# Attention's prologue and first turn in another order, two squares on ScalarE, the reciprocal's transpose two chunks later, layer 1's low parts on VectorE

## The chip, the core and the metric

The kernel runs on one core of a Trainium2 chip. The core has a matrix engine (TensorE, PE in the profile; PEld is its weight load), VectorE (DVE), ScalarE (ACT), GpSimd (POOL) and a queue engine that only issues transfers (SyncE, SP). Each engine works through its own list of instructions in order and waits on semaphores for the others. The metric is device time of one execution in microseconds: the median of the runs.

## What is computed

```
q_n, k_n = rmsnorm(q, g_q), rmsnorm(k, g_k)          # q, k, v: 4 x 12 x 448 x 64
scores = q_n @ k_n^T / sqrt(64)
attn = exp(scores - rowmax);  attn = attn / (rowsum + 1e-9)
x = (attn @ v), heads side by side                   # 1792 x 768
x = ((x @ w_a) * (x @ w_b)) @ w_out                  # layer 0, d_ff 1536
x = (sigmoid(x @ w_gate) * (x @ w_val)) @ w_out      # layer 1, d_ff 1536
```

## The kernel before

Attention works on 24 pairs of heads. For a pair, `load` and `load_r` fetch q and k, `squares` squares them, `mean` sums and averages on VectorE, `rsqrt` takes a logarithm and an exponential on ScalarE, `newton` improves the result on VectorE with three small instructions, and `scale` multiplies q and k with it into `qkn` (n = 1 is k, n = 0 is q, n = 2 the remainders of both, of which q's go to `qrem`). `t_tr` transposes the scaled k (1) and q (0) on TensorE. Every result of the transpose is split in a high and a low part: `k_hi` and `q_hi` are ScalarE copies (k's carries the gain `G`), `k_lo` and `q_lo` VectorE subtractions, and `k_ends` are two small GpSimd copies. `s` makes the scores from high and low parts, three products each, `top` the row maxima on VectorE, `exp` the exponentials and their sums on ScalarE. `x_tr` transposes the exponentials, `x_out` copies them out of PSUM (ScalarE for z = 0, VectorE for z = 1), and `pv` multiplies with v. The normalisation goes round by DRAM: `rsum` takes the reciprocals of the sums on VectorE, `rsum_tr` transposes them on TensorE, `rsum_post` copies the row on ScalarE and stores it (`dr`), `rsum_get` of the next turn loads it back over 64 partitions (`rs`), and `norm` multiplies on VectorE.

No scheduler orders this. The order is written out by hand in three tables: `begin` is the prologue, `turns` is run once for each pair from 1 to 22 with offsets from the pair (so in turn i it makes the scores of pair i, the transposes and products of pair i - 1 and the scaled q and k of pairs i + 1 to i + 4), and `end` closes. An engine's list of instructions is what these tables give it. Squares and scaling of pair 0, and the scaling of pair 1, are on VectorE, of all others on GpSimd. `qkn` has one buffer, `tr` in PSUM three, the scores four. From turn 6 on, `decode` weaves the unpacking of layer 0's weights into each turn; its raw words arrive by SP's queue.

The two layers multiply by a seven-product scheme, every operand again split in high and low. `first_part` makes the gated products, `second_part` the product with w_out: 42 steps k (seven passes of six), each with six chunks on TensorE in layer 0, and behind each chunk a `tick`. A tick calls `step`, which prepares the operands of step k + 3 on VectorE and ScalarE (names d, wh, wl for weights, u, gh, gl for activations), and then takes one task from the list `after`. Behind passes 6 and 7 this list holds three additions (`more`) and three `finish`, whose `split` makes layer 1's operand: the high part by ScalarE, the low part (`xl`, 128x896) by GpSimd. The last two passes of layer 0 write into the same PSUM bank, so the first product of pass 4 has to wait for ScalarE's copy of pass 7 (line 1156).

Of the kernel before, what the change touches and what calls it, by code (L numbers as in the profile page):

```python
# [23 lines left out]
def attention_then_two_gated_mlps(  # L24
# [90 lines left out]
    def attention():  # L115
# [68 lines left out]

        def squares(i):
            d = st[i]
            first = i < 1
# [6 lines left out]
            w = 0 if first else D // 2
            while w >= 32:
                eng.tensor_tensor(out=sq[:, :, 0:w], in0=sq[:, :, 0:w], in1=sq[:, :, w:2 * w], op=ALU.add)
                w //= 2
            d["sq"] = sq if first else sq[:, :, 0:2 * w]
# [72 lines left out]
        def k_hi(i):  # L271
            d = st[i]
            KH, KL = (qk.tile([P, 512], F32R, tag=n, name=n) for n in ("KH", "KL"))
            if i == 0:
                nc.vector.scalar_tensor_tensor(
                    out=G, in0=gg[:, 0:1], scalar=1.0 / float(D) ** 0.5, in1=gg[:, 1:2], op0=ALU.mult, op1=ALU.mult
                )
# [172 lines left out]
        begin = (  # L450
            (load, 0), (load_r, -6), (load_r, -5), (load_r, -4), (load_r, -3), (load_g, 0), (load_r, -2),
            (load, 1), (squares, 0), (mean, 0), (rsqrt, 0), (newton, 0), (load, 2), (scale, 0, 1),
            (load_r, -1), (scale, 0, 0), (load_r, 0), (scale, 0, 2), (t_tr, 0, 1), (k_hi, 0), (squares, 1),
            (mean, 1), (t_tr, 0, 0), (rsqrt, 1), (k_lo, 0), (k_ends, 0), (newton, 1), (load, 3), (load_r, 1),
            (q_hi, 0), (q_lo, 0), (scale, 1, 1), (load_r, 2), (s, 0, 0), (scale, 1, 0), (scale, 1, 2),
            (s, 0, 1), (top, 0, 0), (load_v, 0), (load_v, 1), (t_tr, 1, 0), (squares, 2), (exp, 0, 0), (top, 0, 4),
            (q_hi, 1), (mean, 2), (t_tr, 1, 1), (exp, 0, 4), (q_lo, 1), (rsqrt, 2), (k_hi, 1), (top, 0, 1), (newton, 2),
            (exp, 0, 1), (top, 0, 5), (scale, 2, 1), (k_lo, 1), (k_ends, 1), (exp, 0, 5), (s, 0, 2), (s, 0, 3), (load, 4),
            (scale, 2, 0), (scale, 2, 2), (top, 0, 2), (load_r, 3), (exp, 0, 2), (top, 0, 6), (squares, 3),
            (exp, 0, 6), (top, 0, 3), (t_tr, 2, 1), (t_tr, 2, 0), (exp, 0, 3), (mean, 3), (k_hi, 2), (k_lo, 2),  # L460
            (rsqrt, 3), (q_hi, 2), (newton, 3), (q_lo, 2), (k_ends, 2),
        )
# [788 lines left out]
```

## Time and profile before

| what | us |
|---|---|
| median of three runs (1259.92 to 1262.04) | 1260.2 |
| the profiled execution | 1261.72 |
| its span, first to last instruction | 1259.9 |
| TensorE busy in the span | 1206.6 (96%) |
| VectorE busy | 941.0 (75%) |
| ScalarE busy | 653.0 (52%) |
| GpSimd busy | 183.8 (15%) |

The span is the time from the first to the last instruction, and 1.8 us lie around it. TensorE is busy nearly all the time, so a saving is read from the stretches in which it stands idle or runs at the lower of its clocks; the waits and the timeline show those, with the engine that ended each wait.

### The profile page before, as it was taken

Reading aid. Unit: us, or ns where it says so; the run is one execution under the profiler, and the core shown is the slowest. Engines: PE = TensorE matmul, PEld = TensorE weight load, DVE = VectorE, ACT = ScalarE, POOL = GpSimd, SP = SyncE. Lnnn points to the kernel's source line nnn. Section 1 sums busy time; section 2 is a strip of 40 time slices with the busy share of each in tenths; the row PEclk is TensorE's granted clock in tenths of the full one; section 3 lists DMA queues with packets and bytes.
Section 4 is the critical chain, followed back from the end, with each engine's and each line's share of the span. In section 5 each row is a group of like instructions: output and inputs, shape, how many; then the busy total and the mean of one; then the engine's idle time right before and its main releaser. Section 6 shows DMA issues by size and latency. Waiting matters only on the chain.

```text
span 1259.9 us, 18180 instructions
## 1 busy us (share of the span) xinstructions
PE 1206.6 (96%) x6414; PEld 1016.9 (81%) x6414; DVE 941.0 (75%) x1617; ACT 653.0 (52%) x1267; POOL 183.8 (15%) x250
## 2 busy tenths in 40 slices
PE   4999999999889999999999989989999999999997
PEld 3565665566778888888888878878888888999997
DVE  6787889873986777877557689976787777557583
ACT  3677788773554345334345546544445454445543
POOL 4564557720000000000002022000000000000000
PEclk8899999999899999999999999999999999999999
DMA  5234455425324555653875644123555655577573
GB/s 128 67 111 139 114 143 155 142 83 202 103 86 137 181 168 172 200 166 126 283 244 168 225 157 155 61 94 118 190 168 172 193 155 178 196 274 259 173 254 108
DMA packets 142026, 203.00 MB, mean 161 GB/s; under 512 B 23240, under 2 KB 116592, under 8 KB 141936
## 3 DMA queue, kind: packets, MB, share of 16 engines
q1 hardware_dynamic: 140816, 201.27, 50.6%
q8 instruction: 50, 0.82, 0.3%
q10 hardware_dynamic: 1120, 0.59, 0.2%
q14 instruction: 40, 0.33, 0.1%
HBM read 147.46 MB, written 54.35 MB: 160 GB/s over the span
## 4 chain that ended last, share of the span: by engine, by line
PE 80%; DVE 10%; ACT 4%; issue 2%; DMA 2%; POOL 1%; SPq 0%; ACTq 0%; DVEq 0%; POOLq 0%
PE mm L871 45%; PE mm L1123 10%; PE mm L1133 9%; PE pv L365 5%; PE s L305 5%; PE tr L336 3%; DVE xl L560 2%; DVE nm L311 2%; PE tr L254 1%; PE tr L333 1%; ACT gh L1040 1%; DVE d L630 1%; DMA d<-wd 1%; DVE wl L560 1%; DVE QL L269 1%
## 5 line engine op out<-in xcount | busy, mean ns | idle before, releaser
L871 PE MATMUL mm<-xh,wh 128*128 128x512 f32 (+1 forms) x1008 | 371.1, 368 | 9.5 <-ACT u L923 3.8
L871 PE MATMUL mm<-xl,wh 128*128 128x512 f32 (+1 forms) x1008 | 371.0, 368 | 5.5 <-DVE xl L560 5.5
L871 PE MATMUL mm<-xh,wl 128*128 128x512 f32 (+1 forms) x1008 | 372.0, 369 | 0.0
L560 DVE TENSOR_TENSOR wl<-d,wh 128x384 fp32r<-128x384 f32 x252 | 143.7, 571 | 161.1 <-ACT wh L718 100.2
L871 PEld LDWEIGHTS mm<-xh,wh 128*128 128x128 f32 x1008 | 191.1, 190 | 35.7 <-ACT u L923 4.4
L871 PEld LDWEIGHTS mm<-xl,wh 128*128 128x128 f32 x1008 | 191.1, 190 | 30.2 <-DVE xl L560 7.3
L871 PEld LDWEIGHTS mm<-xh,wl 128*128 128x128 f32 x1008 | 190.7, 189 | 21.3
L718 ACT CAST wh<-d 128x384 fp32r<-128x384 f32 x168 | 85.9, 511 | 167.3 <-DVE d L706 145.9
L1013 ACT CAST wh<-d 128x384 fp32r<-128x384 f32 x84 | 43.2, 514 | 150.0 <-DVE d L1010 54.3
L623 ACT ACTIVATE d<-raw 128x384 f32<-128x384 f32 x140 | 78.1, 558 | 65.0 <-DMA raw<-in_moe_w_a_dram 15.0
L323 ACT ACTIVATE P<-s,nm 128x448 f32<-128x448 f32 x168 | 104.9, 635 | 12.1 <-DVE nm L311 12.1
L311 DVE TENSOR_REDUCE nm<-s 128x1 f32<-128x448 f32 x168 | 97.3, 614 | 7.1 <-PE s L305 7.1
L1133 PE MATMUL mm<-wh,gh 128*128 128x384 f32 x294 | 98.8, 336 | 0.5 <-ACT ah L1156 0.3
L1133 PE MATMUL mm<-wl,gh 128*128 128x384 f32 x294 | 98.6, 335 | 0.0
L1133 PE MATMUL mm<-wh,gl 128*128 128x384 f32 x294 | 98.5, 335 | 0.0
L1123 PE MATMUL mm<-gh,wh 128*128 128x512 f32 x252 | 92.9, 369 | 5.1 <-ACT ah L1156 4.4
L1123 PE MATMUL mm<-gl,wh 128*128 128x512 f32 x252 | 93.4, 371 | 0.0
L1123 PE MATMUL mm<-gh,wl 128*128 128x512 f32 x252 | 93.2, 370 | 0.0
L630 DVE SCALAR_TENSOR_TENSOR d<-d,raw 128x384 uint32<-128x384 uint32 x140 | 81.2, 580 | 10.9 <-ACT d L623 1.3
L560 DVE TENSOR_TENSOR gl<-u,gh 128x896 fp32r<-128x896 f32 x60 | 71.3, 1188 | 18.4 <-ACT gh L1040 18.3
L352 ACT COPY pt<-tr 128x512 f32<-128x512 f32 x96 | 54.8, 571 | 51.6 <-PE tr L336 47.7
L626 DVE SCALAR_TENSOR_TENSOR raw<-raw 128x384 uint32<-128x384 uint32 x140 | 78.2, 558 | 4.1
(148 smaller groups left out, 1948.3 us busy)
## 6 DMA issues: line engine op xcount, KB each, us to landing
gd<-u SPq DMA_DIRECT2D x60, 448.0 KB
u<-gd SPq DMA_DIRECT2D x60, 448.0 KB
d<-wd SPq DMA_DIRECT2D x132, 192.0 KB
raw<-in_moe_w_out_dram SPq DMA_DIRECT2D x48, 384.0 KB
wd<-d SPq DMA_DIRECT2D x72, 192.0 KB
raw<-in_moe_w_a_dram SPq DMA_DIRECT2D x24, 384.0 KB
raw<-in_moe_w_b_dram SPq DMA_DIRECT2D x24, 384.0 KB
raw<-in_moe_w_val_dram SPq DMA_DIRECT2D x23, 384.0 KB
```

The lines of the kernel that those rows point to most:

```text
L305: nc.tensor.matmul(out_, w[e, o:o + P], x[e, m:m + S], start=(n == 0), stop=(n == 2))
L311: nc.vector.tensor_reduce(out=d["nm"][:, t:t + 1], in_=d["ps"][t], axis=AX.X, op=ALU.max, negate=True)
L323: nc.scalar.activation(out=e, in_=d["ps"].pop(t), func=AF.Exp, bias=d["nm"][:, t:t + 1], accum_out=d["sum"][:, t:t + 1])
L365: nc.tensor.matmul(d["pv"][64 * h:64 * h + 64], w, x, start=(j == 0), stop=(j == R), skip_group_check=True)
L560: eng.tensor_tensor(out=lo, in0=t, in1=f32(hi), op=ALU.subtract)
L623: nc.scalar.activation(out=f32(t), in_=f32(high), func=AF.Copy, scale=2.0 ** -112)
L626: nc.vector.scalar_tensor_tensor(out=low, in0=high, scalar=0x80000000, in1=low, op0=ALU.bitwise_and, op1=ALU.bitwise_or)
L630: nc.vector.scalar_tensor_tensor(out=t, in0=t, scalar=3, in1=low, op0=ALU.logical_shift_left, op1=ALU.bitwise_or)
L718: nc.scalar.copy(out=hi, in_=t)
L871: nc.tensor.matmul(ps[:, o:o + size], w[:, P * c:P * c + P], x[:, o:o + size], start=(p in (1, 5) and c == 0 and z == 0), stop=(c == KC - ...
L1123: nc.tensor.matmul(ps[:, o:o + size], w[:, P * un:P * un + P], g[:, o:o + size], start=(p in (1, 5) and f == 0 and z == 0), stop=(f == HF ...
L1133: nc.tensor.matmul(ps[:, o:o + HB], g[:, P * t:P * t + P], w, start=(p in (1, 5) and f == 0 and z == 0), stop=(f == HF - 1 and z == 2), sk ...
```

## The change

- The table `begin` is in another order. The loads of pairs 1 and 2 go out first, the four tiny loads of the gains go from SP's queue to ScalarE's, pair 0 is carried through to its exponentials before pair 1 is scaled, and `G` has a step of its own (`gain`) ahead of q's scaling.
- The first turn has its own table, `first`: without the steps for pair -1 that don't exist, with the preparation of pairs 2 and 3 in other places.
- `squares` of pairs 1 and 3 are on ScalarE (of 2 they stay on GpSimd); the squares of 1 and 2 are kept in a buffer of the exponentials.
- `scale` of pair 1 is on GpSimd.
- In all turns `rsum_tr` stands behind `x_tr` of chunk 2, and `rsum_post` two steps later still. Before they stood ahead of the scores' second half.
- `second_part` of layer 0 takes a task from `after` at every third tick only, and layer 1's low parts are made by VectorE.

```diff
@@ squares @@
-            first = i < 1
-            eng = nc.vector if first else nc.gpsimd
-            sq = nr.tile([P, 14, D], F32, tag="qkn" if first else "sq", name="sq")
+            if i in (1, 2):
+                sq = pp.tile([P, S2], F32, tag="P", name="sq").rearrange("p (s d) -> p s d", d=D)
+            else:
+                sq = nr.tile([P, 14, D], F32, tag="sq" if i else "qkn", name="sq")
...
+            if i in (1, 3):
+                nc.scalar.activation(out=parts[:, :, 0:6], in_=d["qk"], func=AF.Square)
+                nc.scalar.activation(out=parts[:, :, 6], in_=r, func=AF.Square)
+                d["sq"] = sq
+                return
@@ scale @@
-            eng = nc.vector if i < 2 else nc.gpsimd
+            eng = nc.gpsimd if i else nc.vector
@@ turns @@
-            (x_out, -1, 1, 0), (x_tr, -1, 1, 1), (norm, -2), (x_out, -1, 1, 1), (rsum_tr, -1), (s, 0, 2),
-            (rsum_post, -1), (s, 0, 3), (decode, 0, 0), (early_hi, -1), (squares, 3), (early_lo, -1), (x_tr, -1, 2, 0),
-            (top, 0, 2), (x_out, -1, 2, 0), (exp, 0, 2), (x_tr, -1, 2, 1), (top, 0, 6), (exp, 0, 6), (x_out, -1, 2, 1),
+            (x_out, -1, 1, 0), (x_tr, -1, 1, 1), (norm, -2), (x_out, -1, 1, 1), (s, 0, 2),
+            (s, 0, 3), (decode, 0, 0), (early_hi, -1), (squares, 3), (early_lo, -1), (x_tr, -1, 2, 0),
+            (top, 0, 2), (x_out, -1, 2, 0), (exp, 0, 2), (x_tr, -1, 2, 1), (rsum_tr, -1), (top, 0, 6), (exp, 0, 6), (x_out, -1, 2, 1), (rsum_post, -1),
@@ the loop over the turns @@
-            for f, o, *a in turns:
+            for f, o, *a in first if i == 1 else turns:
@@ second_part @@
-            if after:
+            beats.append(k)
+            if after and (l == 1 or len(beats) % 3 == 0):
                 after.pop(0)()
@@ finish @@
-                split(src, hi, lo, nc.gpsimd)
+                split(src, hi, lo, nc.vector)
```

Lines of the changed kernel have other numbers, from 6 to 17 higher. In the rows below, `P` and `P3` are exponentials, `nm` row maxima, `rc` the reciprocals, `ms` the mean squares, `y` their inverse roots.

VectorE in the prologue, from the mean of pair 0 on, before (`ms`, `y` after the first `G` are pair 1's):

```order
L203 TENSOR_REDUCE ms<-sq 128x14
L204 TENSOR_SCALAR ms<-ms 128x14
L219 SCALAR_TENSOR_TENSOR t<-y 128x14
L220 TENSOR_TENSOR t<-t,ms 128x14
L221 SCALAR_TENSOR_TENSOR y<-t,y 128x14
L230 TENSOR_TENSOR qkn<-qk,y 128x384 x2
L243 TENSOR_SCALAR qkn<-rqk,y 128x64
L243 TENSOR_SCALAR qrem<-rqk,y 64x64 x2
L275 SCALAR_TENSOR_TENSOR G<-gg 128x1
L203 TENSOR_REDUCE ms<-sq 128x14
L204 TENSOR_SCALAR ms<-ms 128x14
L288 SCALAR_TENSOR_TENSOR KL<-tr,G,KH 128x448
```

The same place now:

```order
L231 SCALAR_TENSOR_TENSOR y<-t,y 128x14
L240 TENSOR_TENSOR qkn<-qk,y 128x384
L253 TENSOR_SCALAR qkn<-rqk,y 128x64
L253 TENSOR_SCALAR qrem<-rqk,y 64x64 x2
L206 SCALAR_TENSOR_TENSOR G<-gg 128x1
L240 TENSOR_TENSOR qkn<-qk,y 128x384
L294 SCALAR_TENSOR_TENSOR KL<-tr,G,KH 128x448
L279 TENSOR_TENSOR QL<-tr,QH 128x512
L213 TENSOR_REDUCE ms<-sq 128x14
L214 TENSOR_SCALAR ms<-ms 128x14
L317 TENSOR_REDUCE nm<-s 128x1 x2
```

`G` now stands ahead of q's scaling, and the low parts of pair 0 ahead of pair 1's mean; pair 1's scaling is gone from VectorE.

TensorE in a turn, from the transposes of chunk 1 on, before:

```order
L333 MATMUL tr<-ident,P_627 128x2x64
L336 MATMUL tr<-ident,P 128x128 x6
L379 MATMUL tr<-ident,rc 7x128
L305 MATMUL s<-KH,QH 128x448 x2
L305 MATMUL s<-KH,QL 128x448 x2
L305 MATMUL s<-KL,QH 128x448 x2
L305 MATMUL s<-KH,QH 128x448
L305 MATMUL s<-KH,QL 128x448
L305 MATMUL s<-KL,QH 128x448
```

And now:

```order
L339 MATMUL tr<-ident,P_625 128x2x64
L342 MATMUL tr<-ident,P 128x128 x6
L311 MATMUL s<-KH,QH 128x448 x2
L311 MATMUL s<-KH,QL 128x448 x2
L311 MATMUL s<-KL,QH 128x448 x2
L311 MATMUL s<-KH,QH 128x448
L311 MATMUL s<-KH,QL 128x448
L311 MATMUL s<-KL,QH 128x448
L339 MATMUL tr<-ident,P_625 128x2x64
L342 MATMUL tr<-ident,P 128x128 x6
L385 MATMUL tr<-ident,rc 7x128
```

The transpose of the reciprocals (`rc`) now stands behind the scores' second half and the transposes of chunk 2. Its store moves with it in SP's queue. In turn 6, where the first raw weights are loaded, that queue reads before:

```order
L180 DMA v_1375<-in_v_dram 128x2x192
L386 DMA dr_1408<-row_1406 7x128
L612 DMA raw_1414<-in_moe_w_a_dram 128x3x256
L612 DMA raw_1416<-in_moe_w_a_dram 128x3x256
L393 DMA rs_1491<-dr_1408 64x64
```

And now:

```order
L180 DMA v_1373<-in_v_dram 128x2x192
L628 DMA raw_1406<-in_moe_w_a_dram 128x3x256
L628 DMA raw_1408<-in_moe_w_a_dram 128x3x256
L392 DMA dr_1435<-row_1433 7x128
L399 DMA rs_1489<-dr_1435 64x64
```

The two raw loads now stand ahead of the store of the row.

VectorE behind pass 6 of layer 0 (`ah` are the sums, `xl` a low part of layer 1), before:

```order
L1089 TENSOR_TENSOR ah<-ah 128x896 x2
L1010 TENSOR_TENSOR d<-d 128x384
L1028 TENSOR_TENSOR u_8030<-fl,u_8030 128x896
L1089 TENSOR_TENSOR ah<-ah 128x896
L560 TENSOR_TENSOR wl<-d,wh 128x384
L560 TENSOR_TENSOR gl<-u_8030,gh 128x896
L1010 TENSOR_TENSOR d<-d 128x384
```

And now:

```order
L1105 TENSOR_TENSOR ah<-ah 128x896 x2
L1026 TENSOR_TENSOR d<-d 128x384
L1044 TENSOR_TENSOR u_8028<-fl,u_8028 128x896
L576 TENSOR_TENSOR wl<-d,wh 128x384
L576 TENSOR_TENSOR gl<-u_8028,gh 128x896
L1105 TENSOR_TENSOR ah<-ah 128x896
L576 TENSOR_TENSOR xl<-ah,xh 128x896
L1026 TENSOR_TENSOR d<-d 128x384
L1044 TENSOR_TENSOR u_8069<-fl,u_8069 128x896
L576 TENSOR_TENSOR wl<-d,wh 128x384
L576 TENSOR_TENSOR gl<-u_8069,gh 128x896
L576 TENSOR_TENSOR xl<-ah,xh 128x896 x2
```

The third addition goes behind the operands of its step, and three low parts come into VectorE's list over two steps; the same is done behind pass 7.

## Rows read from the trace of the kernel before

**Rows 1.** TensorE's waits, whole run: line, waited for, total, times, longest (us).
```profile
PE tr L379 <- DVE rc L373: 6.1, 8, 2.3
PE mm L1123 <- ACT ah L1156: 4.4, 1, 4.4
```

**Rows 2.** Windows: turns 1, 2, 7; length, PE, PEld, DVE, ACT, POOL, clock, DMA, GB/s.
```profile
27.82:44.47 16.65, 13.66 (x66) 9.03 (x66) 9.35 (x25) 8.41 (x25) 8.82 (x14) 0.69 0.25 73
44.47:55.20 10.73, 10.73 (x74) 6.91 (x73) 8.88 (x21) 7.89 (x24) 6.35 (x11) 1.00 0.19 59
98.15:111.48 13.33, 10.94 (x74) 6.91 (x73) 10.91 (x27) 9.53 (x27) 6.65 (x10) 1.00 0.29 85
```

**Rows 3.** Timeline of TensorE: start, length, line, result, count, idle before and releaser.
```profile
15.84 0.74 PE L305 MATMUL s<-KH,QH 64*128 64x448 f32 x2 [2.86 <-ACT QH L264]
18.26 0.57 PE L305 MATMUL s<-KL,QH 64*128 64x448 f32 x2
...
27.82 0.74 PE L305 MATMUL s<-KH,QH 64*128 64x448 f32 x2
...
45.90 0.33 PE L333 MATMUL tr<-ident,P 128*128 128x128 f32 x1
```

**Rows 4.** Timeline of VectorE and ScalarE in the prologue.
```profile
10.64 1.81 DVE L243 TENSOR_SCALAR qrem<-rqk,y 64x64 f32<-64x64 f32 x2
12.48 0.29 DVE L275 SCALAR_TENSOR_TENSOR G<-gg 128x1 f32<-128x1 f32 x1
...
12.87 0.63 ACT L278 ACTIVATE KH<-tr,G 128x448 fp32r<-128x448 f32 x1 [4.00 <-DVE G L275]
...
19.32 0.51 DVE L243 TENSOR_SCALAR qrem<-rqk,y 64x64 f32<-64x64 f32 x2
```

**Rows 5.** Windows: GpSimd's scaling of pair 3, then its squares of pair 4.
```profile
32.52:35.55 3.03, 0.98 (x7) 0.75 (x7) 3.03 (x7) 2.01 (x6) 2.89 (x5) 0.89 0.00 0
35.59:38.62 3.03, 2.63 (x9) 1.74 (x10) 1.44 (x5) 1.39 (x6) 2.95 (x3) 0.50 0.03 7
```

**Rows 6.** Window: TensorE's granted clock (seventh column) in turn 1.
```profile
28.00:30.00 2.00, 2.00 (x12) 1.63 (x12) 0.00 (x0) 0.00 (x0) 1.92 (x3) 0.50 0.73 211
```

**Rows 7.** Timeline of turns 6 and 7: SP's queue, VectorE, TensorE.
```profile
90.77 0.37 SPq L180 DMA_DIRECT2D v<-in_v_dram  x1
...
93.54 1.04 SPq L612 DMA_DIRECT2D raw<-in_moe_w_a_dram  x2
...
98.72 0.36 DVE L624 TENSOR_SCALAR raw<-raw 128x384 uint32<-128x384 uint32 x1 [2.71 <-DMA raw<-in_moe_w_a_dram]
...
101.38 0.33 PE L333 MATMUL tr<-ident,P 128*128 128x128 f32 x1 [1.74 <-ACT pt L352]
```

**Rows 8.** End of layer 0: two windows beside GpSimd's low parts, then timeline rows.
```profile
737.19:744.85 7.66, 7.66 (x39) 6.84 (x38) 7.66 (x3) 0.95 (x1) 7.33 (x3) 1.00 0.36 114
762.16:769.93 7.77, 7.77 (x39) 6.88 (x39) 7.11 (x5) 2.85 (x4) 6.90 (x3) 1.00 0.06 20
...
746.94 1.09 DVE L560 TENSOR_TENSOR gl<-u,gh 128x896 fp32r<-128x896 f32 x1 [0.54 <-ACT gh L1040]
755.99 2.51 ACT L1156 COPY ah<-mm 128x896 f32<-128x896 f32 x3
756.94 0.80 PE L1123 MATMUL mm<-gh,wh 128*128 128x512 f32 x1 [4.38 <-ACT ah L1156]
```

**Rows 9.** Way of the reciprocals, turns 4 and 5; last, a piece of the chain's start.
```profile
71.73 0.29 SPq L386 DMA_DIRECT2D dr<-row  x1
72.94 1.73 SPq L393 DMA_DIRECT2D rs<-dr  x3
74.22 0.63 ACT L323 ACTIVATE P<-s,nm 128x448 f32<-128x448 f32 x1
81.03 0.62 DVE L400 TENSOR_TENSOR xs<-pv,rs 128x448 f32<-128x448 f32 x1
...
2.52 4.04 DMA rqk<-in_q_dram
```

More of the change, by code (lines that the diff above doesn't have):

```diff
@@ L161, in load_r @@
             e = slice(64 * h, 64 * h + 64)
-            if m == 0:
+            if b not in rem:
                 rem[b] = nat.tile([P, 2, NP, D], F32, tag="rqk", name="rqk", bufs=2)
@@ L170, in load_g @@
             for h in range(2):
-                nc.sync.dma_start(out=gg[64 * h:64 * h + 64, 0:1], in_=g_q.rearrange("(d o) -> d o", o=1))
-                nc.sync.dma_start(out=gg[64 * h:64 * h + 64, 1:2], in_=g_k.rearrange("(d o) -> d o", o=1))
+                nc.scalar.dma_start(out=gg[64 * h:64 * h + 64, 0:1], in_=g_q.rearrange("(d o) -> d o", o=1))
+                nc.scalar.dma_start(out=gg[64 * h:64 * h + 64, 1:2], in_=g_k.rearrange("(d o) -> d o", o=1))
         def load_v(i):
@@ L186, in squares, with gain @@
             d = st[i]
-            first = i < 1
-            eng = nc.vector if first else nc.gpsimd
-            sq = nr.tile([P, 14, D], F32, tag="qkn" if first else "sq", name="sq")
+            if i in (1, 2):
+                sq = pp.tile([P, S2], F32, tag="P", name="sq").rearrange("p (s d) -> p s d", d=D)
+            else:
+                sq = nr.tile([P, 14, D], F32, tag="sq" if i else "qkn", name="sq")
             r = rem[i // NP][:, :, i % NP]
             parts = sq.rearrange("p (n s) d -> p n s d", n=2)
+            if i in (1, 3):
[4 more added lines that the diff above has]
+            eng = nc.gpsimd if i else nc.vector
             eng.tensor_tensor(out=parts[:, :, 0:6], in0=d["qk"], in1=d["qk"], op=ALU.mult)
             eng.tensor_tensor(out=parts[:, :, 6], in0=r, in1=r, op=ALU.mult)
[L194 to L198, printed above, removed]
+            if i:
+                eng.tensor_tensor(out=sq[:, :, 0:32], in0=sq[:, :, 0:32], in1=sq[:, :, 32:64], op=ALU.add)
+            d["sq"] = sq[:, :, 0:32] if i else sq
+        def gain(i):
+            nc.vector.scalar_tensor_tensor(
+                out=G, in0=gg[:, 0:1], scalar=1.0 / float(D) ** 0.5, in1=gg[:, 1:2], op0=ALU.mult, op1=ALU.mult
+            )
         def mean(i):
@@ L225, in scale @@
             y = d["y"].rearrange("p (n s) -> p n s", n=2)
-            eng = nc.vector if i < 2 else nc.gpsimd
+            eng = nc.gpsimd if i else nc.vector
             if n == 1:
@@ L273, in k_hi @@
             KH, KL = (qk.tile([P, 512], F32R, tag=n, name=n) for n in ("KH", "KL"))
[L274 to L277, printed above, removed]
             nc.scalar.activation(out=KH[:, 64:512], in_=d["T", 1][:, 0:S], func=AF.Copy, scale=G)
@@ L450, in attention @@
         begin = (
[L451 to L460, printed above, removed]
@@ L461, in attention @@
-            (rsqrt, 3), (q_hi, 2), (newton, 3), (q_lo, 2), (k_ends, 2),
+            (load, 0), (load_r, -4), (load_r, -3), (load_r, -6), (load_r, -5), (load_g, 0), (load, 1), (load, 2),
+            (load_r, -2), (load_r, -1), (load_v, 0), (squares, 0), (mean, 0), (rsqrt, 0), (squares, 1), (newton, 0),
+            (scale, 0, 1), (scale, 0, 2), (gain, 0), (scale, 0, 0), (load, 3), (load_r, 0), (load_v, 1), (load_r, 1),
+            (t_tr, 0, 1), (k_hi, 0), (t_tr, 0, 0), (k_lo, 0), (q_hi, 0), (q_lo, 0), (k_ends, 0), (squares, 2),
@@ new lines, in attention @@
+            (s, 0, 0), (s, 0, 1), (mean, 1), (rsqrt, 1), (top, 0, 0), (exp, 0, 0), (top, 0, 4), (newton, 1), (exp, 0, 4),
+            (scale, 1, 1), (scale, 1, 2), (scale, 1, 0), (top, 0, 1), (exp, 0, 1), (top, 0, 5), (exp, 0, 5), (s, 0, 2),
+            (mean, 2), (rsqrt, 2), (s, 0, 3), (top, 0, 2), (exp, 0, 2), (newton, 2), (top, 0, 6), (exp, 0, 6),
+            (t_tr, 1, 1), (top, 0, 3), (k_hi, 1), (exp, 0, 3), (t_tr, 1, 0), (k_lo, 1), (q_hi, 1), (q_lo, 1), (k_ends, 1),
+            (scale, 2, 1), (scale, 2, 0), (scale, 2, 2), (squares, 3), (mean, 3), (rsqrt, 3), (load, 4), (load_r, 2),
@@ new lines, in attention @@
+            (load_r, 3),
+        )
+        first = (
+            (x_tr, -1, 0, 0), (x_tr, -1, 0, 1), (s, 0, 0), (s, 0, 1), (top, 0, 0), (x_out, -1, 0, 0), (exp, 0, 0),
+            (top, 0, 4), (exp, 0, 4), (newton, 2), (x_out, -1, 0, 1), (t_tr, 1, 1), (t_tr, 1, 0), (top, 0, 1), (exp, 0, 1),
+            (k_hi, 1), (load, 4), (load_r, 3), (load_v, 1), (k_lo, 1), (q_hi, 1), (q_lo, 1), (k_ends, 1), (scale, 2, 1),
+            (scale, 2, 0), (scale, 2, 2), (top, 0, 5), (rsum, -1), (exp, 0, 5), (x_tr, -1, 1, 0), (x_out, -1, 1, 0),
+            (x_tr, -1, 1, 1), (x_out, -1, 1, 1), (s, 0, 2), (s, 0, 3), (squares, 3),
+            (x_tr, -1, 2, 0), (top, 0, 2), (x_out, -1, 2, 0), (exp, 0, 2), (x_tr, -1, 2, 1), (rsum_tr, -1), (top, 0, 6), (exp, 0, 6),
+            (x_out, -1, 2, 1), (rsum_post, -1), (pv, -1, 0), (top, 0, 3), (t_tr, 2, 1), (exp, 0, 3), (mean, 3), (rsqrt, 3), (x_tr, -1, 3, 0),
+            (k_hi, 2), (newton, 3), (k_lo, 2), (t_tr, 2, 0), (x_out, -1, 3, 0), (q_hi, 2), (q_lo, 2), (k_ends, 2),
@@ L1089, in more @@
             nc.vector.tensor_tensor(out=sums(x, un), in0=sums("a", un), in1=sums(x, un), op=ALU.add)
-        after, finals = [], []
+        after, finals, beats = [], [], []
         def tick(k):
             step(k)
-            if after:
+            beats.append(k)
+            if after and (l == 1 or len(beats) % 3 == 0):
                 after.pop(0)()
```

## The prediction

> **What bounds the kernel now.** I read the busy table first: TensorE works 1206.6 of 1259.9 us, so a saving has to come out of the 53 us in which it stands idle, or out of stretches at its lower clock. Then its waits by line, to see which of the idle pieces the change can reach. Two stand out: 6.1 us in eight waits for the reciprocals `rc`, one of 2.3, and one wait of 4.4 for ScalarE's copy `ah` at the end of layer 0 [rows 1]. The windows by turn come next: turn 2 is 10.73 us long and TensorE is busy for all of it, so an ordinary turn has nothing to give; turn 1 takes 16.65 with 13.66 busy at a mean granted clock of 0.69, turn 7 takes 13.33 [rows 2]. Last the timelines, for what is late at those places. Three places then carry the sum: A, the start up to turn 2; B, the `rc` waits and turn 7; C, the end of layer 0.
>
> **Base.** All terms are taken from the profiled execution, 1261.72 us; it is 1.5 above the median of the runs, 1260.2, so 1.5 comes off at the end.
>
> **A, prologue and first turn.** I follow three marks of before: the first scores at 15.84, the scores of pair 1 at 27.82, the first exponentials' transpose of turn 2 at 45.90 [rows 3].
> First mark: ScalarE's `KH` waits 4.00 us for `G`, which VectorE makes last, at 12.48 to 12.77, behind a pair of `qrem` products that takes 1.81 where the next such pair takes 0.51 [rows 4]. GpSimd squares pair 1 at that time. Now ScalarE makes these squares and `G` stands ahead of q's large scaling. Taking the `qrem` pair at 0.51, it ends at 11.15, and `G` with it; that alone is 1.6 earlier. `KH` then ends near 12.2 (0.63), and `QH` no longer stands behind pair 1's logarithm and exponential on ScalarE; with one more transpose and a copy of about 0.6 (as `KH`) it ends near 13.2. First scores 13.25, 2.6 earlier; 1.6 is the lower bound.
> Second mark: the scores of pair 0's first half keep their 3.0 us (15.84 to 18.83 [rows 3]), so they end at 16.25; their second half runs to 19.4. Pair 1's scaling now goes to GpSimd, 3.03 us by its scaling of pair 3 [rows 5], from 17.0 to 20.05: mostly beside these scores. Two transposes at the slow clock, the copies and pair 1's scores follow: 23.9, 3.9 earlier than 27.82.
> Third mark: 2.3 of before is the wait for `rc` in turn 1 [rows 1], gone with its move. It doesn't come back whole, since GpSimd is next: pair 3's scaling waits for the transposes of pair 2 and their small copies (about 30.5 by the same walk), then come 3.03 of scaling and 3.03 of squares [rows 5], to 36.55, and only then pair 4's mean, whose logarithm stands ahead of the copies that free the transpose buffers. In turn 7 a late VectorE instruction at 98.72 lets the transposes go on at 101.38, 2.66 later [rows 7]; with that, 39.2, 6.7 earlier than 45.90. I take 6.5.
> The ends: TensorE's clock was 0.50 granted (its 1.2 GHz) at 28 to 30 [rows 6] and rose later in turn 1. If it keeps 1.2 GHz until turn 2, the third mark is 41.5, a gain of 4.4; if GpSimd's chain is shorter than I make it, 7.5.
> Costed at nothing: the gains' loads on ScalarE's queue (four issues long before `KH`, which waits 4.00 anyway); ScalarE's squares (under 1 us with ScalarE waiting there; if the cover is gone they delay pair 1's mean by as much, within the bounds); earlier loads in SP's queue.
>
> **B, the reciprocals' transpose.** Seven waits besides turn 1's sum to 6.1 - 2.3 = 3.8 [rows 1]. Two chunks later VectorE has long made `rc`, and the place is filled with scores that wait for nothing new: 3.8 gone. The store of the row moves past two raw loads in SP's queue. Before, SP ended v's load at 91.14 and issued the raw loads at 93.54, behind the store; VectorE waited 2.71 for them until 98.72, and TensorE 1.74 at 101.38 behind that [rows 7]. Now they go out near 91.1, 2.4 earlier, so that 0.3 of VectorE's wait stays and TensorE's 1.74 goes: 3.8 + 1.7 = 5.5. I take 5.0, since VectorE or ScalarE may be late at the next transpose instead. Bounds: 2.4, if half of it returns as waits for ScalarE in the turns that unpack weights; 5.8. What it adds is a small copy in ScalarE's list between exponentials, where TensorE in turns like turn 2 is the bound [rows 2]; where it isn't, this is part of the lower bound.
>
> **C, the end of layer 0.** GpSimd's three low parts take 7.33 us, and beside them three VectorE instructions take 7.66; one of the same size later takes 1.09 and the smaller ones half of that, so 2.2 undisturbed: 5.5 are lost. The second time 6.90 of GpSimd stand beside 7.11 of VectorE, about 5 lost [rows 8]. Now VectorE makes six low parts of about 1.0 each (a price like `gl`'s 1.09): 10.5 - 6 = 4.5 less work. How much of it reaches TensorE? The first loss is partly made up before pass 4, since VectorE waits 0.54 for ScalarE's `gh` at 746.94 already; walking on from there in the new order, the copies of pass 7 start at 754.45 and not at 755.99, so TensorE's 4.38 idle before pass 4 [rows 8] shrinks to about 2.8. Behind it VectorE, without the second 5 us and with three more low parts, reaches the step of 769.93 (where the second window of [rows 8] ends) at 767.7: 2.2 earlier, and it has no gap in which to lose that. I take 2.2. Bounds: 0, if the low parts on VectorE cost the operands as much as GpSimd's did; 4.5, VectorE's whole saving, which is about TensorE's whole idle time.
>
> **Sum.** 6.5 + 5.0 + 2.2 = 13.7: 1261.72 - 13.7 = 1248.0, and 1.5 less for the median: 1246.5.
>
> **The rivals.**
> *The clock stays low.* With less waiting in turn 1 TensorE could still be at 1.2 GHz up to turn 2, where it was at 28 to 30 [rows 6]. A is 4.4: 1248.6. For it: much of turn 1 was at that clock. Against: it rose in turn 1 although TensorE waited there more. Chance 0.10.
> *The waits for `rc` return as waits for ScalarE* in the turns that unpack weights. B is 2.4: 1249.1. For it: ScalarE is busy 9.53 of turn 7's 13.33 and VectorE 10.91 [rows 2], so a 10.9 us turn would leave VectorE no slack. Chance 0.08.
> *C gives nothing:* VectorE's own low parts replace the disturbance. 1248.7, chance 0.04.
> *Slower: the reciprocals come back too late.* This is one mechanism in each turn: `rs` passes by DRAM and `norm` on VectorE needs it at 81.03; before, the row's store went out at 71.73 and the three loads from 72.94 to 74.67 [rows 9], 6.4 us ahead. Now the row is copied behind an exponential that ends at 74.85 [rows 9], so the store is near 75.1 and the loads, by the same distances, end at 78.05: 3.0 us are left, and perhaps 0.6 of slack behind `norm`. If the landing takes up to 3.6 it costs nothing. The nearest rows are higher: 4.04 for a load in the chain [rows 9] and 98.72 - 93.54 = 5.18 for the large raw loads [rows 7]. By 5.18, VectorE would be 1.6 late in some 20 turns, 32 us: 1279. By 4.04 it would be 0.4 and 9 us, which leaves it faster; from 4.24 on it is slower. Against it: the large raw loads are no near likeness of a row, and the loads that depend on the store go out only 1.2 after it, at 71.73 and 72.94 [rows 9]. Chance 0.03.
> The Trainium skill, "DMA: Bandwidth & Descriptors", section "Anatomy of one DMA — SWDGE (gpsimd) path", gives a transfer a fixed cost of about 2.0 us, nearly all of it completion, plus its bytes; the section is about another queue than SP's. By it, as an estimate, `rs` would land 2.3 after its issue, in time by 0.7, and this rival would be priced at nothing. No row before shows its landing, so the chance stays as it is.
> *The change doesn't do what it says:* the new order's gains end in a wait that I don't see, most likely on GpSimd in turns 1 and 2, or its prologue on a load that lands later. 1257 to 1262, chance 0.05.
>
> **How the numbers follow.** The forecast has 0.70, with its own bounds 1242.4 (7.5 + 5.8 + 4.5 off) and about 1252 to 1253 (4.4, 2.4 and nothing would be 1253.4). The first three rivals lie inside. Range 1242.5 to 1252.5; outside it are the slower rival, the last one, and the forecast's own tails. A measurement of this kernel tells about 0.2%, 2.5 us, from no change. Faster by more than that: 0.93, from the forecast, three rivals and part of the last one's lower edge. Within 0.2%: 0.04, the last rival. Slower: 0.03.
>
> **What would show it.** Profile of the changed kernel, A: first scores near 13.3, `G` ending near 11.1, pair 1's scores near 23.9, turn 2's first transpose near 39. B: no wait of TensorE for `rc`, turn 7 near 10.9, raw loads issued near the end of v's load. C: no GpSimd work after attention, low parts of about 1.0 on VectorE, TensorE idle 2 to 3 before pass 4. Wrong would be: a granted clock of 0.5 until turn 2, VectorE's `norm` waiting for `rs`, GpSimd's squares of pair 4 later than 37, or a new idle time of TensorE on ScalarE in the unpacking turns.

## The result, and the profile after

The changed kernel takes 1249.4 us (median of four runs, 1248.4 to 1250.9) against 1260.5: a ratio of 0.9911 with a 95% interval of 0.9894 to 0.9928, 11.1 us less. The prediction said 1246.5 with a range of 1242.5 to 1252.5. The two profiled executions lie further apart than the medians, 1261.72 and 1248.36; the prediction's sum for the latter was 1248.0.

TensorE's waits in the changed kernel, whole run (line, waited for, total, times, longest, us), to be held against [rows 1]:

```profile
PE tr L339 <- ACT pt L358: 5.5, 8, 1.1
...
PE mm L1140 <- ACT ah L1173: 2.9, 1, 2.9
PE tr L342 <- DVE KL L294: 1.8, 1, 1.8
```

The line for `rc` is gone altogether (6.1 before). The wait ahead of pass 4 is 2.9 instead of 4.4. Of the waits in attention two have grown: 1.8 for pair 2's `KL`, 0.4 before, and 5.5 for the copies `pt`, which were 3.0 before.

Windows of turn 1 and turn 7 of the changed kernel (columns as in [rows 2], from the first scores of a turn to those of the next):

```profile
24.93:37.45 12.52, 10.47 (x68) 7.36 (x67) 8.35 (x19) 7.75 (x22) 7.83 (x14) 1.00 0.21 58
92.18:102.89 10.71, 10.71 (x74) 6.87 (x73) 9.53 (x23) 8.48 (x25) 6.66 (x10) 1.00 0.41 111
```

Turn 1 has shrunk from 16.65 to 12.52, although its window is not quite the same one: its table now puts the first transposes ahead of the scores. (The 1.00 for its clock holds from 26.99 on only, as the last section shows.) Turn 7 is down from 13.33 to 10.71, TensorE's own work and no more.

The differences against the kernel before, by the start of the same work in the traces (us), for the changed kernel and for the runs of the next section:

| mark (time before) | changed | e1_start | e2_rc | e3_low | e4_all |
|---|---|---|---|---|---|
| `norm` of turn 3 (59.55) | -5.9 | -5.2 | -4.0 | -0.2 | -5.8 |
| `norm` of turn 7 (105.41) | -8.0 | -6.1 | -5.7 | -0.9 | -7.9 |
| `norm` of turn 15 (192.64) | -9.9 | -6.4 | -7.8 | -0.9 | -9.6 |
| first product of layer 0 (291.93) | -10.6 | -6.0 | -8.6 | -0.8 | -10.1 |
| ahead of pass 4 (750.44) | -11.1 | -5.7 | -8.6 | -0.7 | -9.9 |
| in pass 4 (761.98) | -13.6 | -5.7 | -8.7 | -2.9 | -12.1 |
| last product | -13.8 | -5.6 | -8.8 | -3.0 | -12.1 |

### The profile page after: what moved, and what is told of

It is laid out like the page before. It is cut to its first block, busy times and chain, and to the rows that moved or that the text cites. A ratio compares the mean times of both kernels' runs of the same rounds, so it can differ in the third digit from the quotient of the medians.

```text
span 1246.5 us, 18142 instructions
## 1 busy us (share of the span) xinstructions
PE 1199.8 (96%) x6414; PEld 1014.0 (81%) x6414; DVE 935.9 (75%) x1621; ACT 655.3 (53%) x1271; POOL 157.0 (13%) x240
## 4 chain that ended last, share of the span: by engine, by line
PE 81%; DVE 10%; ACT 4%; issue 2%; DMA 1%; POOL 1%; ACTq 0%; SPq 0%; DVEq 0%; POOLq 0%
PE mm L887 45%; PE mm L1140 10%; PE mm L1150 9%; PE pv L371 5%; PE s L311 4%; PE tr L342 3%; DVE xl L576 2%; DVE nm L317 2%; PE tr L264 1%; PE tr L339 1%; ACT gh L1056 1%; DVE d L646 1%; DMA d<-wd 1%; DVE wl L576 1%; DVE u L1044 1%
## 5 line engine op out<-in xcount | busy, mean ns | idle before, releaser
L576 DVE TENSOR_TENSOR wl<-d,wh 128x384 fp32r<-128x384 f32 x252 | 140.2, 557 | 158.1 <-ACT wh L734 99.9
L576 DVE TENSOR_TENSOR gl<-u,gh 128x896 fp32r<-128x896 f32 x60 | 65.6, 1093 | 20.0 <-ACT gh L1056 19.9
```

Of the source, the lines that this page charges most:

```text
L576: eng.tensor_tensor(out=lo, in0=t, in1=f32(hi), op=ALU.subtract)
```

## The experiments

### The three parts alone

**e1_start** has the new `begin`, `first`, `squares`, `scale` and gains' loads, with the old `turns` and layer boundary.

```diff
-            for f, o, *a in turns:
+            for f, o, *a in first if i == 1 else turns:
```

> The kernel before with the new prologue and first turn alone (with the squares on ScalarE, pair 1's scaling on GpSimd, the gains' loads on ScalarE's queue). Theory of separate parts: the transposes of turn 2 begin near 40, 5.9 earlier than the 45.90 of before, and nothing of it is lost later, so 5.9 us less than before. Rival, that the parts lean on each other (the old place of the reciprocals' transpose in turns 2 and on takes up what the first turn brings): 3 us less or under.

Measured: 1256.9, ratio 0.9963 (0.9952 to 0.9975), 4.3 less. The trace has -5.2 at turn 3 and nothing is given back.

**e2_rc** moves the reciprocals' transpose and the row's copy, in all turns, and changes nothing else.

```diff
-            (x_out, -1, 1, 0), (x_tr, -1, 1, 1), (norm, -2), (x_out, -1, 1, 1), (rsum_tr, -1), (s, 0, 2),
-            (rsum_post, -1), (s, 0, 3),
+            (x_out, -1, 1, 0), (x_tr, -1, 1, 1), (norm, -2), (x_out, -1, 1, 1), (s, 0, 2), (s, 0, 3),
...
-            (x_tr, -1, 2, 1), (top, 0, 6), (exp, 0, 6), (x_out, -1, 2, 1),
+            (x_tr, -1, 2, 1), (rsum_tr, -1), (top, 0, 6), (exp, 0, 6), (x_out, -1, 2, 1), (rsum_post, -1),
```

> The kernel before with the reciprocals' transpose and the copy of the row moved in all turns, nothing else. Theory from the two traces: turn 1 gains 2 to 3 (wait for rc of 2.3), turn 6 gains 2.0, turns 7 to 13 together 2.0 although the list of waits shows hardly any wait there, turns 14 to 20 nothing, the last ones 0.8: 6 to 7.5 us less. Rival, the sum as predicted, by the listed waits alone (3.8 in turns 7 and 14 to 20, 1.7 in turn 6, 2.3 in turn 1): 7.8 less, and gained in turns 14 to 20 and not in 7 to 13.

Measured: 1254.3, ratio 0.9948 (0.9935 to 0.9960), 6.9 less. By the trace it gains 4.0 up to turn 2 (more than the wait of 2.3 that it removes), 1.6 in turn 6, 2.1 in turns 7 to 14, nothing in turns 15 to 20, 0.8 in the last ones. That is the theory's distribution (its turns are numbered one too low at these ends) and not that of the listed waits. Of the 4.0, 0.4 lie ahead of turn 1, where the edit changes nothing (first scores at 15.45 against 15.84), and a part of the rest goes with the clock: during its wait for `rc` the kernel before falls to a granted clock of 0.50, from 34.88 to 41.70, while e2_rc has 1.00 from 29.37 on.

**e3_low** has the low parts on VectorE and the spacing.

```diff
-            if after:
+            if after and (l == 1 or len(beats) % 3 == 0):
...
-                split(src, hi, lo, nc.gpsimd)
+                split(src, hi, lo, nc.vector)
```

> The kernel before with layer 1's low parts on VectorE and a task at every third tick, nothing else. Theory: TensorE's idle before pass 4 falls from 4.4 to 2.8 and the products behind it run 2.2 to 2.6 us earlier to the end: 2.2 to 2.6 less. Rival: given back in layer 1, where TensorE then waits longer for ScalarE: 1 less or under.

Measured: 1258.8, ratio 0.9978 (0.9969 to 0.9987), 2.4 less; 2.2 come at pass 4, and they last to the end. Of these, 1.5 are the shorter idle time; where the other 0.7 come from is told under C below.

**e4_all** is the changed kernel beside them.

> The changed kernel itself once more, beside its parts. Its profiled execution was 13.4 us shorter than that of before, its median 11.1. Theory: run to run they differ by 1 to 2.5 us, and the true difference is 11 to 13.4; the three parts alone then sum to 14 to 16, since turn 1's wait for rc is taken away by two of them. Rival: the difference of the profiled executions is chance and it is 11 or under.

Measured: 1250.4, ratio 0.9911 (0.9899 to 0.9924), 10.8 less. That is the rival: the 13.4 between the two profiled executions were in part chance. The parts alone sum to 4.3 + 6.9 + 2.4 = 13.6; the missing 2.8 is the first turn. By the traces the new start alone brings 5.2 there and the moved transpose 4.0, together 5.9: they take away the same waiting.

### The first turn

**e8_gpsq** puts the squares of pairs 1 and 3 back on GpSimd.

```diff
-            if i in (1, 3):
-                nc.scalar.activation(out=parts[:, :, 0:6], in_=d["qk"], func=AF.Square)
-                nc.scalar.activation(out=parts[:, :, 6], in_=r, func=AF.Square)
-                d["sq"] = sq
-                return
```

> The changed kernel with the squares of pairs 1 and 3 on GpSimd again. Theory as in the prediction: GpSimd's squares of pair 1 slow VectorE's qrem pair (1.81 instead of 0.51) and G, but G has slack of 0.7 in the changed kernel (KH waits for a transpose), so the first scores are 0.6 later; pair 3's squares put 3 us more into GpSimd's chain of the first turn, ahead of its scaling of pair 3: turn 2 is 2 to 3 later in all. Rival: GpSimd has room for them, 0.5 later or less.

Measured: 1255.8, ratio 0.9958 (0.9944 to 0.9972), about 5 more than the changed kernel in e4_all, twice what was expected. Timeline of VectorE, then of TensorE, in this run:

```profile
8.55 1.15 DVE L209 TENSOR_SCALAR ms<-ms 128x14 f32<-128x14 f32 x1
...
10.22 1.03 DVE L224 SCALAR_TENSOR_TENSOR t<-y 128x14 f32<-128x14 f32 x1 [0.53 <-ACT y L217]
...
31.52 0.62 DVE L208 TENSOR_REDUCE ms<-sq 128x14 f32<-128x448 f32 x1 [5.41 <-POOL sq L197]
...
33.37 0.90 PE L259 MATMUL tr<-ident,qkn 128*128 128x128 f32 x3 [5.23 <-ACT pt L353]
```

Beside GpSimd's squares two tiny VectorE instructions of the chain to the first scores take 1.15 and 1.03 (0.18 and 0.17 in the changed kernel): the first scores are at 15.36 instead of 13.65. And pair 3's squares, behind GpSimd's scaling, hold VectorE for 5.41 and so TensorE for 5.23. Turn 2's first products with `rz` begin at 47.90 here, at 47.62 in the kernel before and at 41.75 in the changed one: without ScalarE's squares the new order has no advantage left in the first turn. This trace also has the lower clock for longer, a granted 0.50 from 30.18 to 40.42 (32.44 to 35.85 in e4_all), so not all of the 6 there is the wait itself.

**e7_first** goes on from the changed kernel: it takes the wait for `KL` and the late mean out of the first turn.

```diff
-            ... (top, 0, 1), (exp, 0, 1), (k_hi, 1), (load, 4), (load_r, 3), (load_v, 1), (k_lo, 1), ...
+            ... (k_hi, 1), (k_lo, 1), (top, 0, 1), (exp, 0, 1), (load, 4), (load_r, 3), (load_v, 1), ...
-            ... (exp, 0, 3), (mean, 3), (rsqrt, 3), (x_tr, -1, 3, 0), (k_hi, 2), (newton, 3), (k_lo, 2), ...
+            ... (exp, 0, 3), (x_tr, -1, 3, 0), (k_hi, 2), (k_lo, 2), ... (mean, 3), (rsqrt, 3), (newton, 3), ...
```

> The changed kernel, with two moves in the first turn: pair 2's k copies ahead of an exponential (TensorE waited 1.81 for KL there) and pair 4's mean, logarithm and newton behind pair 3's copies (TensorE waited 1.09 in turn 2 in the first profile, because ScalarE's KH stood behind them). Theory: GpSimd's chain, mean and logarithm are what ends the first turn, so 1 to 2.5 less at turn 2. Rival: GpSimd's scaling of pair 4, which needs pair 4's y, becomes the next wait and gives it back in turn 2: within 0.5.

Measured: 1249.7, ratio 0.9907 (0.9893 to 0.9921), not told apart from the changed kernel. The rival's size was right, its cause in the main another: the wait for `KL` fell from 1.81 to 0.71 and the one of 1.09 vanished, but TensorE ran at its lower clock in the meantime, from 29.21 to 36.04 (e12_best below has the same moves without that). Windows of this run (the granted clock is the seventh column):

```profile
30.00:32.00 2.00, 2.00 (x9) 1.21 (x8) 0.89 (x2) 1.08 (x3) 2.00 (x4) 0.50 0.00 0
...
34.00:36.00 2.00, 2.00 (x8) 0.85 (x8) 1.25 (x3) 2.00 (x7) 1.72 (x3) 0.50 0.00 0
```

### Turn 6 and the turns behind it

**e5_post** leaves the transpose where it was and moves only the copy and store of the row behind the raw loads.

```diff
-            (rsum_post, -1), (s, 0, 3), (decode, 0, 0), (early_hi, -1),
+            (s, 0, 3), (decode, 0, 0), (rsum_post, -1), (early_hi, -1),
```

> The kernel before with only the copy and store of the row moved behind the two raw loads; the transpose of the reciprocals stays where it was. Theory: the raw loads go out 2.4 us earlier in turn 6, VectorE's wait of 2.71 and TensorE's of 1.74 shrink: 1 to 2 less, all of it in turns 6 and 7; turns 1 and 8 to 13 gain nothing, since their waits are for rc itself. Rival: the raw loads land when they do because the transfers ahead of them are slow: nothing, and turn 6's gain belongs to the transpose.

Measured: 1258.6, ratio 0.9982 (0.9973 to 0.9991), 2.4 less. The trace gains 2.56 between `norm` of turns 6 and 7 and nothing before or behind up to layer 0's last passes. (Another 0.7 comes in pass 4, where its edit changes nothing; see C below.) Timeline of SP's queue, for [rows 7]:

```profile
90.67 0.37 SPq L180 DMA_DIRECT2D v<-in_v_dram  x1
91.08 1.00 SPq L612 DMA_DIRECT2D raw<-in_moe_w_a_dram  x2
93.10 0.29 SPq L386 DMA_DIRECT2D dr<-row  x1
```

The raw loads go out 2.4 earlier, behind v's load, and neither VectorE nor TensorE waits there any more. So turn 6's gain needs the row's copy and store behind the raw loads, and not the move of the transpose.

**e6_early** tries the turns that gained nothing, 15 to 20, where GpSimd makes one low part each for layer 0.

```diff
-                nc.gpsimd.tensor_tensor(out=lo, in0=ahead.pop(c), in1=f32(hi), op=ALU.subtract)
+                nc.vector.tensor_tensor(out=lo, in0=ahead.pop(c), in1=f32(hi), op=ALU.subtract)
```

> The changed kernel, with the low parts of layer 0's early operands (one each in turns 14 to 19) on VectorE instead of GpSimd. In the changed kernel turns 14 to 19 take 11.2 to 11.8 us where the turns before take 10.71, and one VectorE instruction of 0.55 takes 1.97 beside GpSimd's 2.1. Theory: this is the bound in these turns, 1.4 lost against 1.1 of added work, and TensorE's waits for ScalarE there (4.4 in all) shrink by 1 to 2.5: 1 to 2.5 less than the changed kernel. Rival: VectorE is simply full there (10.4 to 10.9 busy of 11.3 to 11.8): no gain, or 1 more.

Measured: 1255.7, ratio 0.9950 (0.9936 to 0.9964), 5 more, by the traces about 1.0 in each of five of the six turns and 0.2 in the other: the rival, and worse than it said. In the timeline of VectorE and GpSimd in this run

```profile
211.52 2.08 DVE L434 TENSOR_TENSOR xl<-xst,xh 128x896 fp32r<-128x896 f32 x1 [0.35 <-ACT xh L428]
...
211.51 1.14 POOL L202 TENSOR_TENSOR sq<-sq 128x448 f32<-128x448 f32 x1
```

the low part waits for ScalarE's high part and then lies beside GpSimd's squares, so that it takes 2.08, not the 1.09 that such a part takes alone; it takes 1.73 to 2.08 in five of the turns and 1.09 in the one that loses only 0.2. VectorE, already the fuller engine there, is late for its copies `pt`: TensorE waits 4.6 for them in these turns, for which it did not wait in the changed kernel.

**e12_best** has both edits, of e6_early and e7_first.

> The changed kernel with both: the early low parts on VectorE and the two moves in the first turn. Theory: the two lie in different turns and add up, 2 to 4.5 less than the changed kernel, near 1247. Rival: neither is a bound, within 0.5 of the changed kernel.

Measured: 1254.9, ratio 0.9947 (0.9934 to 0.9961): neither of the two, but e6_early's loss and little of e7_first. In its trace the granted clock does not fall in turn 1; a window of this run, to be held against the second one of e7_first:

```profile
34.00:36.00 2.00, 2.00 (x16) 1.06 (x13) 0.77 (x2) 1.67 (x8) 1.34 (x2) 1.00 0.01 2
```

From the first scores to turn 2's first products with `rz` it takes 39.91 - 13.11 = 26.8 us, the changed kernel 28.1 in both of its traces and e7_first 28.3. So at the higher clock the two moves are worth 1.3 up to there. A turn later 0.8 of it is left, so a part is given back in turn 2, as e7_first's rival had it.

### The end of layer 0

**e10_gplow** puts the low parts back on GpSimd and keeps the spacing; **e9_tick** keeps VectorE and drops the spacing.

```diff
@@ e10_gplow @@
-                split(src, hi, lo, nc.vector)
+                split(src, hi, lo, nc.gpsimd)
@@ e9_tick @@
-            if after and (l == 1 or len(beats) % 3 == 0):
+            if after:
```

> The changed kernel with the low parts on GpSimd again (a task at every third tick stays). Theory: beside each GpSimd low part of about 2.4 us VectorE's operands take two to three times as long, 10.5 us over six of them: the 2.4 of this part are lost, 2 to 3 more than the changed kernel. Rival: spread over three ticks each, GpSimd's work is hidden: 0 to 1 more.

> The changed kernel with a task at every tick again (low parts stay on VectorE). Theory: the low parts' engine is what counts, the spacing puts one addition and one low part behind a step's operands: 0 to 1 more than the changed kernel. Rival: the spacing is what lets pass 7's copies start early: all of the 2.4 lost.

Measured: e10_gplow 1252.7, ratio 0.9933 (0.9921 to 0.9946), 2.4 more than e4_all (3.3 by the traces over this stretch); e9_tick 1248.2, ratio 0.9900 (0.9887 to 0.9914), 2.2 less than it, though the intervals overlap. For e9_tick neither theory nor rival had a gain. Timeline of VectorE and GpSimd in e10_gplow, with TensorE ahead of pass 4, and then TensorE's wait there in e9_tick:

```profile
732.19 2.48 DVE L1026 TENSOR_TENSOR d<-d 128x384 f32<-128x384 f32 x1
734.60 3.01 DVE L1044 TENSOR_TENSOR u<-fl,u 128x896 f32<-128x896 f32 x1
...
732.06 4.59 POOL L576 TENSOR_TENSOR xl<-ah,xh 128x896 fp32r<-128x896 f32 x2 [4.32 <-ACT xh L579]
...
748.61 0.79 PE L1140 MATMUL mm<-gh,wh 128*128 128x512 f32 x1 [5.15 <-ACT ah L1173]
```

```profile
PE mm L1140 <- ACT ah L1173: 2.2, 1, 2.2
```

Beside two GpSimd parts, instructions of 0.55 and 1.08 take 2.48 and 3.01, as in [rows 8]. The Trainium skill ("SBUF — State Buffer", section "SBUF: two separate sides") has VectorE and GpSimd share one pair of ports, which an instruction of GpSimd, or one of VectorE with two inputs in SBUF, locks for its whole length; the rows agree: each of the two is 1.9 longer, and one GpSimd part takes 2.3. TensorE's idle time is 5.15 here and 2.85 with VectorE's low parts. The spacing brings nothing: without it TensorE's idle is shorter (2.2 against 2.9), and by the traces e9_tick is 2.0 better than the changed kernel over this stretch. The other 1.3 of that is TensorE's clock, which does not fall there in e9_tick (C below); whether the spacing has a part in that, one trace does not settle.

### The slower rival

**e11_late** moves the reciprocals' transpose and the row to the end of the turn.

```diff
-            ... (x_tr, -1, 2, 1), (rsum_tr, -1), ... (x_out, -1, 2, 1), (rsum_post, -1),
+            ... (x_tr, -1, 2, 1), ... (x_out, -1, 2, 1),
...
-            ... (x_out, -1, 3, 0), (q_hi, 2), (q_lo, 2), (k_ends, 2),
+            ... (rsum_tr, -1), (x_out, -1, 3, 0), (q_hi, 2), (q_lo, 2), (k_ends, 2), (rsum_post, -1),
```

> The changed kernel with the reciprocals' transpose and the copy of the row moved once more, to the end of the turn, 2.5 to 3 us later. It measures how long the loads of rs take to land, which no profile showed: in the changed kernel they are issued until 82.73 and norm takes them at 85.82 without a wait; here they would be issued until about 85.5. Theory, landing about 2 us after the last issue: norm waits 1 to 2 us, which VectorE's slack in the turns before 6 hides in part: 5 to 25 more. Rival, landing within 1: nothing.

Measured: 1286.9, ratio 1.0201 (1.0187 to 1.0215), some 36 more than the changed kernel, above the theory's range. Not all of that is `rs`: at its new place the transpose also waits for a buffer in PSUM (28.6 us in 20 waits for `pt`), so the price of the late load alone is not settled by this run. Its landing is. Timeline of SP's queue and VectorE in e11_late, and then in the changed kernel at the one place where `norm` waits:

```profile
52.21 1.73 SPq L399 DMA_DIRECT2D rs<-dr  x3
...
56.42 0.62 DVE L406 TENSOR_TENSOR xs<-pv,rs 128x448 f32<-128x448 f32 x1 [1.46 <-DMA rs<-dr]
```

```profile
123.84 1.73 SPq L399 DMA_DIRECT2D rs<-dr  x3
...
129.24 0.62 DVE L406 TENSOR_TENSOR xs<-pv,rs 128x448 f32<-128x448 f32 x1 [0.34 <-DMA rs<-dr]
```

From the end of the last issue to `norm` it is 56.42 - 53.94 = 2.5 us; most of the waits for this load in e11_late give 2.3 to 2.8, one 3.85, and the one in the changed kernel 129.24 - 125.57 = 3.7. The prediction's sentence on the Trainium skill ("DMA: Bandwidth & Descriptors", section "Anatomy of one DMA — SWDGE (gpsimd) path") estimated 2.3; the trace agrees at the low end and not at the high one.

## Why the prediction was right, point by point

**The base.** The sum of 13.7 is close to what the two profiled executions show, 13.4; that it is so close is in part luck, for e4_all's profiled execution, the same kernel, is 11.7 below the one before. What failed is the step behind it, "1.5 less for the median". Over many more runs the kernel before has medians of 1261.1 to 1261.6, so its profiled execution stood 0.1 to 0.7 above them, not 1.5; and the profiled one of the changed kernel was the fastest of its runs. Most of the 2.9 us between 1246.5 and 1249.4 lies there. e4_all, e9_tick and e10_gplow are 1.0 to 1.2 behind the first trace of the changed kernel by the 400th product of layer 0, and were at most 0.5 behind at the first one: that trace was lucky there.

**A, 6.5: measured 5.9.** The first mark came at 13.65, not 13.25. `G` was in time (ended 11.34, forecast 11.1), but it was no longer what `KH` waits for. Timeline of ScalarE:

```profile
12.04 0.64 ACT L284 ACTIVATE KH<-tr,G 128x448 fp32r<-128x448 f32 x1 [1.77 <-PE tr L269]
```

TensorE's transposes of k set this start, and the walk had left them out. In the kernel before they end at 11.54, in time for the forecast; here at 12.00, because q's remainder landed later in this trace and VectorE's whole chain with it. VectorE's square of it, before and then now:

```profile
6.76 0.29 DVE L193 TENSOR_TENSOR sq<-rqk 128x128 f32<-128x128 f32 x1 [0.45 <-DMA rqk<-in_q_dram]
```

```profile
7.22 0.29 DVE L200 TENSOR_TENSOR sq<-rqk 128x128 f32<-128x128 f32 x1 [0.71 <-DMA rqk<-in_q_dram]
```

With the new prologue this square starts at 6.68 to 7.24 in the traces here, and the first scores at 13.11 to 13.68 wherever ScalarE squares pair 1. The second mark came at 24.93, not 23.9 (24.13 in e4_all, where the products get faster earlier). At the third mark the named next bound, GpSimd's chain, was right. Timeline of GpSimd, VectorE, ScalarE and TensorE in turn 1:

```profile
36.48 1.14 POOL L202 TENSOR_TENSOR sq<-sq 128x448 f32<-128x448 f32 x1
...
37.65 0.62 DVE L213 TENSOR_REDUCE ms<-sq 128x14 f32<-128x448 f32 x1 [2.44 <-POOL sq L202]
...
38.94 0.62 ACT L284 ACTIVATE KH<-tr,G 128x448 fp32r<-128x448 f32 x1
...
40.03 0.33 PE L339 MATMUL tr<-ident,P 128*128 128x128 f32 x1 [1.09 <-ACT pt L358]
```

Squares to 37.6 (forecast 36.55), mean, `KH`, transposes at 40.03 (39.2). Mis-told was where the gain comes from. The prediction names ScalarE's squares as a cause of the earlier `G`, and else only as a cost of nothing; e8_gpsq shows that 5 to 6 hang on them, most of it by pair 3's. And turn 1's `rc` wait was booked at 2.3; e2_rc alone gains 4.0 with it, and the new start alone 5.2.

**The clock rival, 0.10.** In the first trace TensorE was at its lower clock up to 26.97, by the length of its products, and at 2.4 GHz by the granted clock for the rest of turn 1; in e4_all, the same kernel, it was already faster at pair 1's scores (24.13), and then at 0.61 and 0.54 in 32 to 36. Yet turn 2 began at the same time (its first products with `rz` at 41.75 and 41.67): the first trace was 0.8 behind at pair 1's scores already, and TensorE waits 1.09 for GpSimd's chain in it. In e7_first, where that wait is gone, the lower clock takes its place. No trace of the changed kernel kept the lower clock up to turn 2, so the rival's own price was not measured.

**B, 5.0: measured 4.7, and the sum is right for the wrong reasons.** The term of 3.8 for seven listed waits brought almost nothing where six of them are, in turns 15 to 21: there 3.2 of waits for `rc` and 0.7 for `pt` became 4.1 of waits for `pt`. That is the prediction's second rival, though only in the later ones of the turns that unpack weights; turns 7 to 14 unpack them too and show nothing of it. The term for the raw loads, 1.7, measured 2.0, and 2.56 in e5_post. And turns 7 to 14 gained 1.9, though the list shows but one wait there, of 0.65. TensorE's timeline in turn 9 of before, and then in turn 8 of the changed kernel:

```profile
126.39 0.82 PE L336 MATMUL tr<-ident,P 128*128 128x128 f32 x6
127.32 0.27 PE L379 MATMUL tr<-ident,rc 128*7 128x128 f32 x1
```

```profile
109.42 0.82 PE L342 MATMUL tr<-ident,P 128*128 128x128 f32 x6
110.07 0.27 PE L385 MATMUL tr<-ident,rc 128*7 128x128 f32 x1
```

From start to start it is 0.93 before and 0.65 now. The wait for `rc` was there in four of these turns, 0.25 to 0.3 each, but the modelled end of the transposes ahead of it covers all but 0.1, which the view of waits and the idle column don't list. With 0.8 in turn 7, counted in the same way, that is the 1.9. These turns are 10.74 to 11.02 long before, 10.71 or 10.72 now.

**C, 2.2: measured 2.5 (2.2 in e3_low and e4_all), and 0.9 of it has another cause.** The first step of the walk held. Timeline of ScalarE and TensorE:

```profile
743.37 2.51 ACT L1173 COPY ah<-mm 128x896 f32<-128x896 f32 x3
...
744.32 0.79 PE L1140 MATMUL mm<-gh,wh 128*128 128x512 f32 x1 [2.85 <-ACT ah L1173]
```

The copies start 12.6 earlier than in [rows 8], 1.5 beyond the 11.1 gained by then, as worked out; TensorE's idle is 2.85 (forecast about 2.8), 1.5 less. e10_gplow shows that the engine is the cause, e9_tick that the spacing is not. The rest of the 2.2 the prediction gave to VectorE, which gets to its next step earlier. But TensorE waits for no one in the first products of pass 4, before or after: it runs at its lower clock there, for a shorter time. Windows of the kernel before, whose pass 4 begins at 756.94, then of the changed kernel (744.32) and of e9_tick (744.87); the granted clock is the seventh column:

```profile
758.00:760.00 2.00, 2.00 (x7) 1.81 (x6) 2.00 (x4) 0.73 (x2) 0.00 (x0) 0.50 0.96 321
760.00:762.00 2.00, 2.00 (x7) 1.75 (x7) 2.00 (x3) 2.00 (x4) 0.00 (x0) 0.52 1.01 329
```

```profile
744.00:746.00 2.00, 1.69 (x4) 1.40 (x5) 2.00 (x3) 1.88 (x3) 0.00 (x0) 0.50 0.82 239
748.00:750.00 2.00, 2.00 (x11) 1.77 (x11) 1.72 (x3) 1.34 (x2) 0.00 (x0) 1.00 0.94 308
```

```profile
746.00:748.00 2.00, 2.00 (x12) 1.77 (x11) 2.00 (x4) 0.73 (x2) 0.00 (x0) 1.00 0.97 323
```

The first 13 products of the pass take 5.0 us before, 4.1 in the changed kernel's first trace, 4.3 in e4_all and 2.8 in e9_tick. In e5_post, whose layer 0 is that of the kernel before, they take 4.3 too. So a part of the measured size is the clock of the run, and the sum came out right with a step that brought nothing here.

**The slower rival, 0.03.** Its point of decision was about 3.6 us of landing for a cost and 4.24 for slower. Measured landings are 2.3 to 2.8 mostly and 3.7 at times. The changed kernel stands close to that edge, closer than the chance of 0.03 makes one think: in turns 3 to 6 `norm` starts 2.4 to 3.1 after the end of the last issue, and one place already waits 0.34.

## What to carry to other kernels

A list of waits is not the whole of what a wait costs: where a turn is longer than the engine's own work in a turn that waits for nothing, compare the starts of the same two instructions in both. Before two savings at one place are added, ask whether they end the same wait; here 5.2 and 4.0 made 5.9. And an engine that is "free" for a helper's work is not free for its neighbour: beside GpSimd's work VectorE's instructions took up to six times as long here (0.17 became 1.03 in the prologue, 0.55 became 2.48 at the layer boundary), while ScalarE's squares cost nothing that was seen. Last, read the clock behind a wait before its shortening is booked: the same 13 products took 5.0, 4.1 or 2.8 us.

## What was not expected of the hardware

The granted clock of the same program's same stretch differs from run to run. In turn 1 of the changed kernel it is 0.50 (1.2 GHz) from 32.44 to 35.85 in e4_all, behind a stretch (26 to 30) in which TensorE was busy for 1.67 of 4.00 us. The first trace has such a stretch too (28 to 32, busy for 1.95) and no fall behind it. At the start of pass 4 it is 0.50 for 6.8 us in the kernel before, for 3.4 us in both traces of the changed kernel and not at all in e9_tick. What sets it in either case was not tried.

And a granted clock of 1.00 in the windows does not by itself mean fast products, for the view shows 1.00 also where the trace holds no record of the clock. In the changed kernel's first trace the window of 20 to 22 us has 1.00, and yet a product of 448 columns takes 0.57 to 0.58 up to 26.6 and 0.37 from 26.97 on. The record of that trace begins at 26.99, with 1.00, just there; in the kernel before it begins at 21.22. Ahead of the record the length of the products tells the clock, and the column does not.
